# First batch in six transfers on two queues, feed-forward by rows of x, and casts of v in four pieces: an attention and GEGLU kernel

## The chip, the cores and the metric

One NeuronCore of a Trainium2 chip. The metric is the time of one execution in microseconds (us), as the device reports it. A profile is one execution with the hardware profiler on; its span is about 1.8 us shorter than the time reported for that execution. TensorE is PE in the profile, VectorE DVE, ScalarE ACT, GpSimd POOL, SyncE SP.

## The reference, cut to what matters

```python
q_s = softmax(q, over the 64 columns of a head)
k_s = softmax(k, over the 576 positions)        # written out with max and exp
kv  = einsum('bhsd,bhse->bhde', k_s, v)
x   = einsum('bhsd,bhde->bhse', q_s, kv)         # 8 batches, 8 heads, 576 positions, 64
x   = x.transpose(0, 2, 1, 3).reshape(4608, 512)
out = (gelu(x @ w_gate) * (x @ w_val)) @ w_out   # 512 -> 1536 -> 512, all float32
```

## The kernel before

The kernel works batch by batch. While PE does the feed-forward of batch b, the other engines prepare batch b+1: exp on ScalarE, sums and multiplies ("norm") on VectorE, the cast of v to 16 bits on GpSimd, and between feed-forward tiles PE does transposes (`unit_t`), K times V (`unit_kv`) and the products that give x (`unit_x`). Batch 0 has nothing to hide behind, so its start is exposed. Parts that the change touches (cuts marked `# ...`):

```python
def load(src, nm, b, h0, h1, n0):
    # ...
    for t in range(2):                       # even partitions, odd partitions
        nc.sync.dma_start(out=tiles[key][t:P:2, h0:h1, ...], in_=src[b, h0:h1]...)

def cast_v(b, h0, h1, eng="pool"):           # float32 -> float16
    copy_on(eng, v16_b[b % 2][:, :, h0:h1, 0:D]..., tiles[("v", b)][:, h0:h1, :]...)

def norm_mul(b, hp, eng="dve"):              # 128 x 640, both inputs in SBUF
    (nc.gpsimd if eng == "pool" else nc.vector).tensor_tensor(out=e, in0=e, in1=rrq..., op=ALU.mult)

def ffn_first(xt, after):                    # tiles by rows of x: rows 0,1 of all tiles, then 2, then 3
    # ...                                    # used for batch 1 only

for src, nm, n0 in ((q, "q", 1), (k, "k", 0), (v, "v", 0)):
    for h0 in (0, 4):
        load(src, nm, 0, h0, h0 + 4, n0)     # 12 transfers, all from SyncE; then the weights
# ...
warm_pe(14); norms of batch 0; unit_t(0, 0); warm_pe(4)
cast_v(0, 0, 4, "dve"); unit_t(0, 1); unit_kv(0, 0); warm_pe(2)
cast_v(0, 4, 6, "act"); cast_v(0, 6, 8, "dve")
unit_x(0, 0); unit_x(0, 1); unit_kv(0, 1); ... unit_x(0, 2); unit_x(0, 3)
```

`warm_pe(n)` runs n matmuls on zeros; it is meant to keep PE's clock up.

The softmax here doesn't subtract the row's maximum and nothing guards it: scores larger than these inputs give would overflow.

Of the kernel before, what the change touches and what calls it, by code (L numbers as in the profile page):

```python
# [18 lines left out]
def kernel(  # L19
# [10 lines left out]
    nc = tc.nc  # L30

    B, H, S, D = q.shape
# [65 lines left out]
    def load(src, nm, b, h0, h1, n0):  # L98
        key = (nm, b)
        if key not in tiles:  # L100
            tiles[key] = ldp.tile([P, H, NC * D], f32, name=f"{nm}t", tag="ld")
        for t in range(2):
            nc.sync.dma_start(  # L103
                out=tiles[key][t:P:2, h0:h1, n0 * D:NC * D],
                in_=src[b, h0:h1].rearrange("h (m n) d -> m h (n d)", n=NT)[
                    :, :, (4 * t + n0) * D:(4 * t + NC) * D])
# [10 lines left out]
    def copy_on(eng, dst, src):  # L117
        if eng == "pool":
            nc.gpsimd.tensor_copy(out=dst, in_=src)  # L119
        elif eng == "act":  # L120
            nc.scalar.copy(out=dst, in_=src)  # L121
        else:
            nc.vector.tensor_copy(out=dst, in_=src)  # L123

    def cast_w(nm, c, eng="pool"):
        dst = (wg_sb if nm == "wg" else wv_sb)[:, :, WCH[c]:WCH[c + 1]]
        copy_on(eng, dst, wst[(nm, c)])
# [11 lines left out]
    def exp(nm, b, h0=0, h1=H, n0=0, parts=((1, NC), (0, 1))):  # L139

        dst = (ek_b if nm == "k" else eq_b)[b % 2]
        for c0, c1 in parts if nm == "k" else ((n0, NC),):
            nc.scalar.activation(  # L143
                out=dst[:, c0:c1, h0 * D:h1 * D].rearrange("p n (h d) -> p h n d", d=D),
                in_=tiles[(nm, b)][:, h0:h1, c0 * D:c1 * D].rearrange("p h (n d) -> p h n d", d=D),
                func=ACTF.Exp, bias=kbias[:, 0:1] if c1 == 1 else 0.0)

    def cast_v(b, h0, h1, eng="pool"):
        copy_on(eng, v16_b[b % 2][:, :, h0:h1, 0:D].rearrange("p n h d -> p h n d"),
                tiles[("v", b)][:, h0:h1, :].rearrange("p h (n d) -> p h n d", d=D))  # L150

# [14 lines left out]
    def norm(b, hp, eng="dve", n0=0):  # L166
        norm_sum(b, hp, n0)
        norm_mul(b, hp, eng)
# [16 lines left out]
    def unit_kv(b, g):  # L185
        pskv = ps_att.tile([P, 2, 2 * VW], f32, name="pskv", tag="att")
        for j in range(2):
            hp = 2 * g + j
            for n in range(NC):
                nc.tensor.matmul(  # L190
                    pskv[:, j, :], ek_b[b % 2][:, n, hp * P:(hp + 1) * P],
                    v16_b[b % 2][:, n, 2 * hp:2 * hp + 2, 0:VW],
                    start=(n == 0), stop=(n == NC - 1))
        rck = att.tile([P, 2], f32, name="rck", tag="rck")
        nc.vector.reciprocal(out=rck, in_=pskv[:, :, D])
        for j in range(2):
            kv_sb = att.tile([P, 2, D], f16, name="kv_sb", tag="kv", bufs=12)
            nc.vector.scalar_tensor_tensor(  # L198
                out=kv_sb,
                in0=pskv[:, j, :].rearrange("p (h e) -> p h e", e=VW)[:, :, 0:D],  # L200
                scalar=rck[:, j:j + 1], in1=mask, op0=ALU.mult, op1=ALU.mult)
            st[(b, "kv", 2 * g + j)] = kv_sb

    def get_eqt(b):
        if (b, "eqt") not in st:
            st[(b, "eqt")] = att.tile([P, HP, S], f16, name="eqt", tag="eqt")
        return st[(b, "eqt")]

    def unit_t(b, g, eng="dve"):
        eqt = get_eqt(b)  # L210
        pst = ps_att.tile([P, 2, MAIN], f16, name="pst", tag="att")
        for j in range(2):
            hp = 2 * g + j
            for n in range(NM):
                nc.tensor.transpose(  # L215
                    pst[:, j, n * P:(n + 1) * P],
                    eq_b[b % 2][:, n + 1, hp * P:(hp + 1) * P], ident)
        copy_on(eng, eqt[:, 2 * g:2 * g + 2, 0:MAIN], pst)
# [14 lines left out]
    def get_xt(b):  # L233
        if (b, "xt") not in st:
            st[(b, "xt")] = att.tile([P, HP, MAIN], f16, name="xt", tag="xt")
        return st[(b, "xt")]

    def unit_x(b, hp, eng="act", big=False):
        xt = get_xt(b)
        psx = (ps_big if big else ps_att).tile([P, MAIN], f32, name="psx",  # L240
                                               tag="mm" if big else "att")
        nc.tensor.matmul(psx, st[(b, "kv", hp)].rearrange("p h e -> p (h e)"),  # L242
                         st[(b, "eqt")][:, hp, 0:MAIN], start=True, stop=True)
        copy_on(eng, xt[:, hp, :], psx)
# [8 lines left out]
    def warm_pe(n):  # L253
        ps = ps_big.tile([P, 512], f32, name="pswarm", tag="mm")
        for _ in range(n):
            nc.tensor.matmul(ps, ident, warm, start=True, stop=True)
# [5 lines left out]
    def mm_gv(ps, w, xt, fi, cis):  # L262
        for ci in cis:
            nc.tensor.matmul(ps, w[:, ci, fi * P:(fi + 1) * P], xt[:, ci, :],  # L264
                             start=(ci == 0), stop=(ci == HP - 1))

    def gate(psg, psv):
        gl = ffn.tile([P, 512], f32, name="gl", tag="gl")
        nc.scalar.activation(out=gl, in_=psg, func=ACTF.Gelu)  # L269
        ht = htp.tile([P, 512], f16, name="ht", tag="ht")  # L270
        nc.vector.scalar_tensor_tensor(  # L271
            out=ht, in0=psv, scalar=_H_SCALE, in1=gl, op0=ALU.mult, op1=ALU.mult)
        return ht
# [8 lines left out]
    def ffn_first(xt, after):  # L282

        ps = []
        for fi in range(len(after)):
            psg = ps_big.tile([P, 512], f32, name="psg", tag="mm")
            mm_gv(psg, wg_sb, xt, fi, range(0, 2))
            psv = ps_big.tile([P, 512], f32, name="psv", tag="mm")
            mm_gv(psv, wv_sb, xt, fi, range(0, 2))
            ps.append((psg, psv))  # L290
            for f in after[fi]:
                f()
        for fi, (psg, psv) in enumerate(ps):
            mm_gv(psg, wg_sb, xt, fi, [2])
            mm_gv(psv, wv_sb, xt, fi, [2])
        hts = []
        for fi, (psg, psv) in enumerate(ps):
            mm_gv(psg, wg_sb, xt, fi, [3])
            mm_gv(psv, wv_sb, xt, fi, [3])
            hts.append(gate(psg, psv))  # L300
        return hts
# [46 lines left out]


    for src, nm, n0 in ((q, "q", 1), (k, "k", 0), (v, "v", 0)):  # L350
        for h0 in (0, 4):
            load(src, nm, 0, h0, h0 + 4, n0)
    for c in range(NW):
        load_w_gv(c)
    for c in range(3):
# [17 lines left out]
    exp("q", 0, 4, 8, 1)  # L373
    exp("k", 0, 0, 4)
    exp("k", 0, 4, 8)
    warm_pe(14)
    norm(0, 0, "dve", 1)
    norm(0, 1, "pool", 1)
    norm(0, 2, "dve", 1)
    norm(0, 3, "pool", 1)  # L380
    unit_t(0, 0, "dve")
    warm_pe(4)
    cast_v(0, 0, 4, "dve")
    unit_t(0, 1, "dve")
    unit_kv(0, 0)
    warm_pe(2)
    cast_v(0, 4, 6, "act")
    cast_v(0, 6, 8, "dve")
    unit_x(0, 0, "act", True)
    unit_x(0, 1, "act", True)  # L390
    unit_kv(0, 1)
    cast_w("wg", 0, "pool")
    cast_w("wv", 0, "pool")
    unit_x(0, 2, "act", True)
    unit_x(0, 3, "dve", True)
    preload(ACTF.Gelu)
    for c in range(1, NW):
# [6 lines left out]
    FI, NS = 0, 1  # L404
    plan = {}

    def at(b, kind, i, *fns):
# [12 lines left out]
       L(preload, ACTF.Gelu))  # L420
    first1 = [[L(unit_kv, 1, 1), L(unit_t, 1, 1)], [L(unit_x, 1, 2, "act")],
              [L(unit_x, 1, 3, "dve")]]

    at(1, FI, 2, L(unit_trem, 1))
    at(1, FI, 3, L(exp, "q", 2), L(norm, 2, 0))
# [35 lines left out]
    def ride(b, kind, i):  # L461
        for fn in plan.get((b, kind, i), []):
            fn()

    for b in order:
        xt = get_xt(b) if b < B else xtr
        hts = []
        fi0 = 0
        if b == 1:
            hts = ffn_first(xt, first1)  # L470
            fi0 = 3
            ride(b, FI, 2)
        for fi in range(fi0, NFI):
            hts.append(ffn_fi(xt, fi))
            ride(b, FI, fi)
        if b == 0:
            psys = []
            for ns in range(4):
                psys.append(ps_big.tile([P, C], f32, name="psy", tag="mm"))
                mm_out(psys[ns], hts, ns, range(0, NFI // 2))  # L480
                ride(b, NS, ns)
            for ns in range(4):
                mm_out(psys[ns], hts, ns, range(NFI // 2, NFI))
                evac(b, ns, psys[ns])
                ride(b, NS, 4 + ns)
        else:
            for ns in range(4):
                psy = ps_big.tile([P, C], f32, name="psy", tag="mm")
                mm_out(psy, hts, ns, range(NFI))
                evac(b, ns, psy)  # L490
                ride(b, NS, ns)
# [30 lines left out]
```

## Time and profile before

| | before |
|---|---|
| time, three runs | 333.1 us median (332.79 to 333.62) |
| profiled execution | 332.57 us, span 330.8 |
| PE busy | 317.1 us, 96% |
| first feed-forward matmul | 18.39 us |
| rate of the transfers, 2 to 10 us | 263 GB/s, 388 later |

The lines themselves stand in the prediction. Reading hint: a PE matmul's record lasts 0.379 us, yet a row of 12 takes 2.59 us on the chain of waits, 0.216 each.

### The profile page before, as it was taken

To read this page: it belongs to the slowest core of one execution; us is meant where nothing else is said; L and a number is where in the kernel's file an instruction comes from. 1 tells how busy PE (TensorE), PEld (TensorE's weight loads), DVE (VectorE), ACT (ScalarE), POOL (GpSimd) and SP (SyncE) were. 2 spreads that over 40 slices of the span, in tenths; PEclk is the share of its full clock that TensorE was granted. 3 is DMA by queue.
4 is the path that set the end of the run, shared out by engine and by line. 5 is a ranking of instruction groups with operands and counts; after the bars stand their busy time and mean duration, and the time that the engine had idled before them with its cause. 6 is when DMAs were issued, how large, how long until landed. Compare 5 with 4: busy or idle time off the path is not lost.

```text
span 330.8 us, 4451 instructions
## 1 busy us (share of the span) xinstructions
PE 317.1 (96%) x1700; PEld 151.9 (46%) x1700; DVE 183.9 (56%) x327; ACT 146.7 (44%) x196; POOL 41.0 (12%) x40
## 2 busy tenths in 40 slices
PE   7699999997999999999999999999999999999994
PEld 2334444444455544544454445444544444444441
DVE  4743375499579736962599238832983234333331
ACT  3553564896353582349134932474243033103300
POOL 1377462211000200020002000200000000000000
PEclk9799999999999999999999999999999999999999
DMA  6999999970177015900491029301100110040002
GB/s 189 356 383 391 402 393 391 395 263 0 63 247 294 2 53 164 387 2 0 164 389 53 2 106 355 144 0 65 63 0 2 63 63 2 0 110 17 4 32 95
DMA packets 38453, 50.49 MB, mean 153 GB/s; under 512 B 2208, under 2 KB 34208, under 8 KB 38432
## 3 DMA queue, kind: packets, MB, share of 16 engines
q1 hardware_dynamic: 38288, 50.08, 42.7%
q8 instruction: 13, 0.21, 0.3%
q10 hardware_dynamic: 144, 0.13, 0.1%
q14 instruction: 8, 0.07, 0.1%
HBM read 40.76 MB, written 9.44 MB: 152 GB/s over the span
## 4 chain that ended last, share of the span: by engine, by line
PE 77%; DMA 9%; DVE 5%; ACT 3%; SPq 2%; issue 2%; POOL 1%; DVEq 0%; ACTq 0%; POOLq 0%
PE psy L308 26%; PE psg L264 23%; PE psv L264 22%; DMA wvst<-in_moe_w_val_dram 4%; DMA qt<-in_q_dram 3%; PE pskv L190 2%; DVE eq L163 2%; DMA kt<-in_k_dram 2%; PE psx L242 2%; PE pst L215 2%; DVE rq L156 1%; SPq L103 1%; ACT eq L143 1%; DVE ht L271 1%; ACT L143 1%
## 5 line engine op out<-in xcount | busy, mean ns | idle before, releaser
L269 ACT ACTIVATE gl<-psg 128x512 f32<-128x512 f32 x108 | 64.0, 598 | 140.3 <-PE psg L264 130.3
L271 DVE SCALAR_TENSOR_TENSOR ht<-psv,gl 128x512 f16<-128x512 f32 x108 | 73.8, 688 | 65.3 <-PE psv L264 61.0
L264 PE MATMUL psg<-xt,wg_sb 128*128 128x512 f16 x384 | 100.1, 379 | 0.7 <-ACT xt L121 0.5
L264 PE MATMUL psv<-xt,wv_sb 128*128 128x512 f16 x384 | 99.5, 379 | 0.1
L308 PE MATMUL psy<-wo_sb,ht 128*128 128x512 f16 x432 | 95.8, 379 | 0.0
L264 PEld LDWEIGHTS <-wv_sb 128*128 128x128 f16 x432 | 42.2, 98 | 51.9 <-issue 1.4
L308 PEld LDWEIGHTS <-ht 128*128 128x128 f16 x432 | 41.7, 98 | 48.4 <-DVE ht L271 0.2
L264 PEld LDWEIGHTS <-wg_sb 128*128 128x128 f16 x432 | 40.9, 98 | 45.0 <-issue 1.8
L342 DVE TENSOR_SCALAR yo<-psy 128x512 f32<-128x512 f32 x31 | 21.2, 687 | 48.6 <-PE psy L308 48.6
L119 POOL CAST v<-vt 128x2560 f16<-128x2560 f32 (+1 forms) x7 | 14.9, 2123 | 148.2 <-DMA vt<-in_v_dram 140.6
L156 DVE TENSOR_REDUCE rq<-eq 128x10 f32<-128x640 f16 (+1 forms) x32 | 25.4, 793 | 9.5 <-ACT eq L143 9.3
L163 DVE TENSOR_TENSOR eq<-eq,rrq 128x640 f16<-128x640 f16 (+1 forms) x27 | 26.0, 963 | 0.9
L121 ACT CAST xt<-psx 128x512 f16<-128x512 f32 x27 | 15.1, 587 | 16.8 <-PE psx L242 16.8
L143 ACT ACTIVATE eq<-qt 128x2560 f16<-128x2560 f32 (+1 forms) x9 | 18.5, 2051 | 4.7 <-DMA qt<-in_q_dram 4.6
L143 ACT ACTIVATE ek<-kt 128x2048 f16<-128x2048 f32 (+1 forms) x10 | 15.6, 1560 | 3.7 <-DMA kt<-in_k_dram 3.7
L215 PE MATMUL pst<-ident,eq 128*128 128x128 f16 x128 | 11.1, 226 | 4.9 <-DVE eq L163 2.8
L215 PEld LDWEIGHTS <-eq 128*128 128x128 f16 x128 | 8.7, 100 | 9.9 <-POOL eq L163 2.7
L190 PE MATMUL pskv<-v,ek 128*128 128x130 f16 x160 | 12.0, 220 | 1.2 <-DVE v L123 1.1
L190 PEld LDWEIGHTS <-ek 128*128 128x128 f16 x160 | 10.4, 97 | 4.7 <-issue 1.5
L264 PE MATMUL psg<-xtr,wg_sb 128*128 128x512 f16 x48 | 12.3, 379 | 0.0
L264 PE MATMUL psv<-xtr,wv_sb 128*128 128x512 f16 x48 | 12.3, 379 | 0.0
L242 PE MATMUL psx<-eqt,kv_sb 128*128 128x512 f16 x32 | 10.8, 380 | 1.1 <-DVE kv_sb L198 0.9
(52 smaller groups left out, 131.8 us busy)
## 6 DMA issues: line engine op xcount, KB each, us to landing
qt<-in_q_dram SPq DMA_DIRECT2D x14, 640.0 KB, 6.8
kt<-in_k_dram SPq DMA_DIRECT2D x12, 640.0 KB, 8.2
vt<-in_v_dram SPq DMA_DIRECT2D x12, 640.0 KB, 9.7
out_dram<-yo SPq DMA_DIRECT2D x14, 512.0 KB, 3.1
wost<-in_moe_w_out_dram SPq DMA_DIRECT2D x6, 512.0 KB, 8.8
kt<-in_k_dram SPq DMA_DIRECT2D x8, 320.0 KB, 6.8
vt<-in_v_dram SPq DMA_DIRECT2D x8, 320.0 KB, 6.6
wgst<-in_moe_w_gate_dram SPq DMA_DIRECT2D x5, 512.0 KB, 7.4
```

The lines of the kernel that those rows point to most:

```text
L121: nc.scalar.copy(out=dst, in_=src)
L143: nc.scalar.activation(out=dst[:, c0:c1, h0 * D:h1 * D].rearrange("p n (h d) -> p h n d", d=D), in_=tiles[(nm, b)][:, h0:h1, c0 * D:c1 * D ...
L156: nc.vector.reduce_sum(rq, e, axis=mybir.AxisListType.X)
L163: (nc.gpsimd if eng == "pool" else nc.vector).tensor_tensor(out=e, in0=e, in1=rrq.unsqueeze(-1).to_broadcast((P, n, 2, D)), op=ALU.mult)
L190: nc.tensor.matmul(pskv[:, j, :], ek_b[b % 2][:, n, hp * P:(hp + 1) * P], v16_b[b % 2][:, n, 2 * hp:2 * hp + 2, 0:VW], start=(n == 0), sto ...
L215: nc.tensor.transpose(pst[:, j, n * P:(n + 1) * P], eq_b[b % 2][:, n + 1, hp * P:(hp + 1) * P], ident)
L242: nc.tensor.matmul(psx, st[(b, "kv", hp)].rearrange("p h e -> p (h e)"), st[(b, "eqt")][:, hp, 0:MAIN], start=True, stop=True)
L264: nc.tensor.matmul(ps, w[:, ci, fi * P:(fi + 1) * P], xt[:, ci, :], start=(ci == 0), stop=(ci == HP - 1))
L269: nc.scalar.activation(out=gl, in_=psg, func=ACTF.Gelu)
L271: nc.vector.scalar_tensor_tensor(out=ht, in0=psv, scalar=_H_SCALE, in1=gl, op0=ALU.mult, op1=ALU.mult)
L308: nc.tensor.matmul(psy, hts[fi][:, ns * P:(ns + 1) * P], wo_sb[:, fi, :], start=(fi == 0), stop=(fi == NFI - 1))
L342: nc.vector.tensor_scalar(out=yo, in0=psy, scalar1=1.0 / _H_SCALE, scalar2=None, op0=ALU.mult)
```

## The change

The intent: bring in batch 0 sooner, start the feed-forward when two rows of x are there, and let VectorE through between GpSimd's casts of v. Its core:

```diff
-            nc.sync.dma_start(
+            eng = nc.scalar if b == 0 and t == 1 else nc.sync
+            eng.dma_start(
@@ cast_v
+        if eng == "pool" and h1 - h0 > 2:
+            for h in range(h0, h1, 2):
+                cast_v(b, h, h + 2)
+            return
@@ start
-        for h0 in (0, 4):
-            load(src, nm, 0, h0, h0 + 4, n0)
+        load(src, nm, 0, 0, H, n0)
-    warm_pe(14)
+    warm_pe(16)
-    warm_pe(4)
+    warm_pe(6)
     cast_v(0, 0, 4, "dve")
+    cast_v(0, 4, 6, "act")
     unit_t(0, 1, "dve")
+    cast_v(0, 6, 8, "pool")
     unit_kv(0, 0)
-    warm_pe(2)
-    cast_v(0, 4, 6, "act")
-    cast_v(0, 6, 8, "dve")
+    unit_kv(0, 1)
     unit_x(0, 0, "act", True)
     unit_x(0, 1, "act", True)
-    unit_kv(0, 1)
     ...
-    unit_x(0, 2, "act", True)
+    unit_x(0, 2, "dve", True)
@@ feed-forward
+    first = {0: [[], []], 1: first1}
-        if b == 1:
-            hts = ffn_first(xt, first1)
+        if b in first:
+            hts = ffn_first(xt, first[b])
```

More of the change, by code (lines that the diff above doesn't have):

```diff
@@ L468 @@
         fi0 = 0
-        if b == 1:
-            hts = ffn_first(xt, first1)
-            fi0 = 3
-            ride(b, FI, 2)
+        if b in first:
+            hts = ffn_first(xt, first[b])
+            fi0 = len(hts)
+            ride(b, FI, fi0 - 1)
         for fi in range(fi0, NFI):
```

## The prediction

> **What bounds the kernel now.** I read the page first. TensorE (PE) is busy nearly everywhere except at the very start, and the clock drops in one early slice; the DMA engines are full from the second slice to the seventh.
>
> ```profile
> PE   7699999997999999999999999999999999999994
> PEclk9799999999999999999999999999999999999999
> GB/s 189 356 383 391 402 393 391 395 263 0 63 247 294 2 53 164 387 2 0 164 389 53 2 106 355 144 0 65 63 0 2 63 63 2 0 110 17 4 32 95
> ```
>
> So time can come from few places. I asked for busy time in chosen stretches (time, then PE busy, PEld, DVE, ACT, POOL, clock, DMA share, GB/s). PE idles 2.2 us in 2 to 10, 1.5 in 10 to 15, 0.8 in 48 to 61, 1.9 in 61 to 92, 0.4 in 160 to 195, and almost nothing between these:
>
> ```profile
> 2.00:10.00 8.00, 5.79 (x22) 2.21 (x21) 3.86 (x10) 2.33 (x4) 1.04 (x1) 0.99 0.92 263
> 10.00:15.00 5.00, 3.47 (x24) 1.86 (x23) 3.41 (x6) 2.91 (x4) 1.04 (x1) 0.67 1.07 374
> 39.40:48.00 8.60, 8.51 (x46) 4.07 (x45) 5.06 (x10) 6.34 (x5) 4.79 (x5) 1.00 1.06 397
> 61.00:92.00 31.00, 29.13 (x166) 14.16 (x164) 22.63 (x38) 21.98 (x24) 4.37 (x2) 1.00 0.41 153
> 160.00:195.00 35.00, 34.58 (x195) 16.88 (x193) 22.41 (x37) 16.98 (x22) 2.33 (x1) 1.00 0.40 143
> ```
>
> Third, the chain of waits (start, length, what). Up to 39.5 us it runs through transfers, not through PE; then through the normalisation of batch 1 on VectorE and GpSimd; later it is PE, with two long VectorE pieces:
>
> ```profile
> 4.87 5.92 DMA kt<-in_k_dram
> 12.03 6.00 DMA wvst<-in_moe_w_val_dram
> 18.36 7.80 DMA wvst<-in_moe_w_val_dram
> 29.25 10.23 DMA qt<-in_q_dram
> 46.33 1.27 POOL eq L163
> 73.60 2.99 DVE eq L163
> 176.15 2.68 DVE eq L163
> ```
>
> Last, the timeline around the start and around those pieces. The rows below are, in order: the last cast of v for batch 0 (two), the first feed-forward matmuls, and the collision near 74 us with PE's wait for it.
>
> ```profile
> 15.08 0.73 ACT L121 CAST v<-vt 128x640 f16<-128x640 f32 x1 [1.89 <-DMA vt<-in_v_dram]
> 15.88 0.88 DVE L123 CAST v<-vt 128x640 f16<-128x640 f32 x1
> 18.39 1.32 PE L264 MATMUL psg<-xt,wg_sb 128*128 128x512 f16 x4
> 73.58 2.32 POOL L119 CAST v<-vt 128x2560 f16<-128x2560 f32 x1 [10.53 <-DMA vt<-in_v_dram]
> 73.60 2.98 DVE L163 TENSOR_TENSOR eq<-eq,rrq 128x640 f16<-128x640 f16 x1
> 76.64 0.40 PE L215 MATMUL pst<-ident,eq 128*128 128x128 f16 x4 [1.67 <-DVE eq L163]
> ```
>
> The same VectorE multiply takes 0.82 us everywhere else, so it lost 2.16 us here and 1.85 us at 176.15, each time to a GpSimd cast of v that started just before it (73.58, and 175.81). PE lost 1.67 us the first time and 0.42 us the second.
>
> **What the Trainium skill says.**
> 1. "SBUF — State Buffer", section "Who interferes with whom": VectorE and GpSimd share one port pair as an exclusive lock held for a whole instruction; a tensor_tensor with both inputs in SBUF contends with a GpSimd instruction that reads SBUF. The trace agrees: 2.98 us against 0.82 us, ending 0.6 us after the cast.
> 2. "DMA: Bandwidth & Descriptors", section "Issuing engines are not separate DMA queues": transfers from any engine run on the same 16 DMA engines; a second issuer saves only issue time. SyncE spends 0.77 us on the first issue and 0.61 to 0.62 on an unhindered one, here.
> 3. The same page, section "Queues, rings and completion order": a DMA engine takes turns between rings by packets, so two queues share rather than add. No run before shows two loading queues.
> 4. "TensorE: Matmul & The Clock Gate", section "Part 1: The HAM clock gate (the "warmup" mystery)": the clock halves after an idle window of about 3.4 us. The trace agrees in size: clock 0.93 in 9 to 10, 0.50 in 10 to 13, 0.87 in 13 to 14, about 3.4 us in all, following PE's gaps after its first 14 warming matmuls.
>
> **The change part by part.**
>
> *(a) Transfers.* Twelve issues become six, three on SyncE and three on ScalarE. For q, k and v each, the two cover odd and even partitions with all eight heads. Issue time for the batch falls from about 8.6 us on SyncE (0.74 to 9.3) to about 2 us on each queue. But issuing did not bind: transfers land 4 to 6 us after issue, so a backlog always waited. What is lost is rate: 263 GB/s from 2 to 10 us against 388 later, although the engines count as busy (0.92). In windows of one microsecond it is 276, 221 and 239 from 5 to 8, then 393 at 12. At 388 GB/s the 2.1 MB moved in those 8 us (8 times 263) take 5.4 us, so 2.6 us is the ceiling; about 1 us of it is the first transfers starting, which stays. I give the two queues half of the rest, some 0.8 us, because a slow packet in one ring need not hold up the other; that share is a guess. So v, 3.67 MB in all, should have landed at about 14.2 instead of just before 15.08. The price is that halves by heads are gone: the first exp on q, at 4.82 before, waits for all of q, say 6.5 to 7.5. The second exp, at 7.89 before, then follows 1.06 after the first, so its end, 8.95, hardly moves.
>
> *(b) Casts of batch 0's v.* All of v lands at once, and three engines cast: VectorE four heads (0.83), ScalarE two (0.73), GpSimd two (0.72, the size that it cast in batch 1 at 50.12). Before, VectorE's second cast sat behind a GpSimd weight cast, 0.88 us for half the size of one that took 0.83. Now GpSimd and VectorE meet again under the lock: together about 1.55 us.
>
> *(c) First two tiles by rows of x.* They start when two rows of x are there. Before, fi 0 started at 18.39 and fi 1 at 20.41, 2.02 us apart instead of 1.73 (8 matmuls of 0.216), so at most 0.3 us is to be had. After v lands: VectorE cast 0.93, ten matmuls 0.74, reciprocal and two products 0.8, product with queries and copy about 1.0, so first feed-forward matmul at about 3.4 us; before, 18.39 less 15.0 is also 3.4. Third tile: 16 matmuls later, 6.9 us after v instead of 22.14 less 15.0, 7.1. From the lock in (b) I take 0 to 0.7 back. So PE gains what v gains, about 0.8, plus 0.2, less 0.4: 0.6 us.
>
> *(d) Does it survive?* At 46.33 to 47.60 GpSimd multiplies batch 1's q, and PE starts the transposes on it at 47.64 after waiting 0.26 us. That piece hangs on q of batch 1, landed at 39.48 on a saturated stream. PE cannot pass it earlier than the stream advances, so (c) alone would be swallowed; what passes is the smaller of PE's and the stream's gain. The stream's is the 0.8 of (a). So 0.6 passes.
>
> *(e) GpSimd by head pairs.* Each whole-batch cast of 2.32 us becomes four of 0.72 (2.88, on an engine busy 12%). VectorE waits for one piece, up to 0.7, not 2.2. PE had 0.5 us of slack at 74 us (2.16 lost, 1.67 passed on) and 1.4 at 176 (1.85, 0.42). So nearly all of 1.67 plus 0.42 comes back: 2.0, less 0.2 for the piece that remains: 1.8 us. That VectorE gets in between two GpSimd instructions I take from the start: its cast at 15.88 ended at 16.76, between GpSimd casts started 15.80 and 16.53 (the latter took 0.69, not 0.61).
>
> *(f) Warming.* 20 small warm-up matmuls become 22; two between unit_kv calls go. On PE's idle time; no cost of their own.
>
> Sum: 0.6 plus 1.8 is 2.4 us less. I take off 0.3 for the rivals: 2.1, so 331.0 us.
>
> **The rivals.**
> - *The cold start stays.* The slow packets of the first 10 us belong to the memory, not to the queue, and two queues only interleave. For: the engines counted busy at 221 GB/s. Then (a), (c), (d) give 0 to 0.2, and (e) alone makes 331.3.
> - *The split casts hold on to the port.* If GpSimd runs its four back to back and VectorE gets no turn, VectorE would wait up to 2.9 us. Against: 15.88 above. Then 0.5 us worse at 74, and 333.0 or a little more.
> - *The clock.* Half clock in the window in which the feed-forward starts costs 1.2 to 1.7 us at the start. For: the warm-up inside the wait for v is gone and more waits stand together. Against: 22 warming matmuls. I give it 1 in 8; it would make 332.3.
> - *The collision moves by luck.* Cast and multiply met within 0.02 us at 74; in batches cast at 107.75, 142.44 and 211.78 VectorE was first and lost nothing. Any shift of the start could undo the 74 us stall without the split. This gives the same 331, for another reason.
> - *Two queues win all.* 1.6 us off the transfers and no lock: 329.8.
>
> **Range and chances.** The sum gives 331.0; the cold-start rival 331.3; the good case 329.8, with up to 0.5 for noise (three runs spread 0.8). Bad: 333.0. Range 329.5 to 333.1. Faster by over 2% needs under 326.4, a gain of 6.7, more than all idle PE time named above after 15 us plus the transfers' ceiling: 0.02. Slower by over 2% needs 339.8, several stalls at once: 0.01.
>
> **What would show it.** (a) the last cast of v in batch 0 starts near 14.2, GB/s in 2 to 10 rises above 290. (c) third tile's first matmul near 21.5. (d) q of batch 1 lands 0.5 to 1 us before 39.48. (e) no VectorE multiply of 640 columns over 1.6 us, PE idle in 61 to 92 under 0.5. Wrong if v lands after 14.9, if a multiply still takes 2.5, or if the clock shows 0.5 after 16 us.

## The result, and the profile after

| | before | after |
|---|---|---|
| time | 332.95 us median of 4 (332.37 to 333.62) | 329.31 us median of 4 (328.81 to 329.83) |
| profiled execution | 332.57, span 330.8 | 329.83, span 328.0 |
| PE busy | 317.1 | 317.6 |

The ratio is 0.989, 95% interval 0.9865 to 0.9915. Ratios here are the mean time of one kernel's fast runs over that of the other's of the same rounds, so not quite the ratio of the medians. The gain is 3.6 us where 2.1 was predicted; 329.31 lies 0.2 under the low end of the range.

The page after, the same three rows in 40 slices. PE's 7 in the tenth slice is gone. The clock's second slice has fallen from 7 to 5, and the transfers run at 236 and 375 GB/s in the first two slices instead of 189 and 356:

```profile
PE   7699999999999999999999999999999999999994
PEclk9599999999999999999999999999999999999999
GB/s 236 375 386 393 400 393 388 398 221 0 64 304 242 3 65 192 352 2 15 177 389 29 2 128 377 105 0 79 50 0 2 64 64 2 2 109 19 2 32 96
```

Busy time by stretch after (time, PE busy, PEld, DVE, ACT, POOL, clock, DMA share, GB/s). The stretch 61 to 92 lost 1.87 us of PE before and loses 0.33 now; 160 to 195 lost 0.42 and loses nothing. But 2 to 15 us is no better for PE, at clock 0.50 in the second row:

```profile
2.00:10.00 8.00, 5.56 (x19) 2.10 (x17) 2.58 (x6) 3.49 (x4) 0.00 (x0) 0.96 0.96 330
10.00:15.00 5.00, 3.65 (x17) 1.74 (x15) 4.67 (x9) 3.53 (x5) 2.95 (x3) 0.50 1.10 370
...
61.00:92.00 31.00, 30.67 (x177) 14.91 (x176) 20.76 (x37) 23.53 (x24) 4.25 (x6) 1.00 0.39 144
...
160.00:195.00 35.00, 35.00 (x197) 17.18 (x195) 20.78 (x38) 17.21 (x23) 3.34 (x4) 1.00 0.40 143
```

The chain of waits after (start, length, what). It no longer follows the transfers to 39.5 us: it leaves them at 6.7, goes through the preparation of batch 0, partly through six warm-up matmuls at half clock, and is on PE from there. The long VectorE piece at 73 us is 1.42, not 2.99:

```profile
0.74 5.97 DMA qt<-in_q_dram
...
10.52 1.05 POOL eq L168
...
12.23 2.56 PE pswarm L261 x6
...
39.40 7.77 PE psy L313 x36
...
73.25 1.42 DVE eq L168
```

The timeline after, at the start and at the former collision. All casts of v begin by 14.07, against 15.88 before. VectorE's takes 1.35 us where 0.83 is its own time, GpSimd's 1.31 for 0.72: they share the port, first with GpSimd's multiply that ran until 14.13. At 71.93 GpSimd casts in four pieces, and the multiply at 73.25 waits for one of them only; the eight transposes of PE follow with 0.27 us lost:

```profile
13.44 0.73 ACT L122 CAST v<-vt 128x640 f16<-128x640 f32 x1
13.46 1.35 DVE L124 CAST v<-vt 128x1280 f16<-128x1280 f32 x1
14.07 1.31 POOL L120 CAST v<-vt 128x640 f16<-128x640 f32 x1
...
18.39 0.72 PE L269 MATMUL psg<-xt,wg_sb 128*128 128x512 f16 x2
...
71.93 3.31 POOL L120 CAST v<-vt 128x640 f16<-128x640 f32 x4 [9.99 <-PE psv L269]
...
73.25 1.41 DVE L168 TENSOR_TENSOR eq<-eq,rrq 128x640 f16<-128x640 f16 x1
...
74.23 0.89 PE L220 MATMUL pst<-ident,eq 128*128 128x128 f16 x8
```

### The profile page after: what moved, and what is told of

Same layout as the page of the kernel before. It is cut to its first block, busy times and chain, and to the rows that moved or that the text cites. A ratio compares the mean times of both kernels' runs of the same rounds, so it can differ in the third digit from the quotient of the medians.

```text
span 328.0 us, 4481 instructions
## 1 busy us (share of the span) xinstructions
PE 317.6 (97%) x1702; PEld 153.0 (47%) x1702; DVE 180.7 (55%) x327; ACT 146.0 (44%) x195; POOL 46.3 (14%) x59
## 4 chain that ended last, share of the span: by engine, by line
PE 90%; DVE 4%; ACT 2%; DMA 2%; issue 1%; POOL 0%; DVEq 0%; ACTq 0%; POOLq 0%
PE psy L313 28%; PE psg L269 27%; PE psv L269 26%; PE pskv L195 3%; PE pst L220 2%; PE psx L247 2%; DMA qt<-in_q_dram 2%; DVE rq L161 1%; PE pswarm L261 1%; DVE eq L168 1%; DVE ht L276 1%; ACT eq L144 1%; PE pstr L232 1%; DVE kv_sb L203 0%; ACT L274 0%
## 5 line engine op out<-in xcount | busy, mean ns | idle before, releaser
L120 POOL CAST v<-vt 128x640 f16<-128x640 f32 x26 | 20.5, 828 | 140.9 <-DMA vt<-in_v_dram 63.9
L168 DVE TENSOR_TENSOR eq<-eq,rrq 128x640 f16<-128x640 f16 (+1 forms) x27 | 22.8, 845 | 0.9
L124 DVE COPY eqt<-pst 128x1024 f16<-128x1024 f16 x16 | 10.8, 678 | 0.9 <-PE pst L220 0.9
```

The source lines that it names most:

```text
L120: nc.gpsimd.tensor_copy(out=dst, in_=src)
```

## The experiments

Runs e1 to e4 shared one chip and 11 runs of before (332.7 us median, 331.07 to 333.99); e5 to e16 ran on another chip, in three sessions that share most of their 12 runs of before (332.54 us median, 331.83 to 333.93). e13 to e16 are single executions. All gave a correct result. The theory: the port's and the start's gains add, each of about 2 and 1 us. Rivals: the collision was luck of the trace; the transfers' rate belongs to the memory; the clock hides the start's gain.

### e1: the changed kernel again

No edit.

> The changed kernel once more, for its spread and for a second profile of its start. Main theory (start and split add, and the start depends on which clock window the first feed-forward matmuls meet): 3 to 4 us under before; the profile may show clock 0.5 in a different stretch than 9.6 to 16.4, and if it is back at 1.0 by 14 us, the output matmuls of batch 0 start about 1 us before 39.24. Rival (the first measurement was a lucky draw): 2 to 2.7 us, as the span of the first profile (2.75).

328.97 us (328.73 to 329.22), ratio 0.9888 (0.9865 to 0.9911). The size stands: 3.7 us, and it was not a lucky draw. In this trace the half clock came later and was shorter (12.35 to 15.76 us instead of 9.37 to 16.20), and the first feed-forward matmul came at 17.92 instead of 18.39.

### e2: the split alone

```diff
# kernel before, plus
+        if eng == "pool" and h1 - h0 > 2: ... cast_v(b, h, h + 2) ...
```

> Kernel before with nothing but the cast of v by head pairs on GpSimd. Main theory: 1.6 to 2.4 us under before, PE idle in 61 to 92 falls from 1.9 to about 0.3, no 640-column multiply over 1.5 us; nothing changes before 60 us. Rival (the collision at 74 us is luck of the profiled run, absent in most runs): under 1 us. Rival (GpSimd keeps the port through its four pieces): slower than before.

330.75 us, ratio 0.9944 (0.9918 to 0.9969), so 1.9 us. The port's part is real without any change of the start. Its profile happened to be its slowest run (331.63), and shows what the clock can do to a start. The rows are the stretches 10 to 15 and 15 to 20 us (the clock is the third number from the end), then the first feed-forward matmul, then the multiply:

```profile
10.00:15.00 5.00, 3.16 (x17) 1.74 (x18) 2.81 (x6) 2.91 (x4) 1.04 (x1) 0.50 1.07 368
15.00:20.00 5.00, 4.35 (x26) 2.73 (x27) 2.38 (x8) 1.80 (x3) 2.58 (x4) 0.58 1.08 334
```

```profile
20.14 1.32 PE L268 MATMUL psg<-xt,wg_sb 128*128 128x512 f16 x4
...
75.17 1.39 DVE L167 TENSOR_TENSOR eq<-eq,rrq 128x640 f16<-128x640 f16 x1
```

PE started at 20.14 instead of 18.39, 1.75 us later, with the same program at that place. Not all of this is the clock: the last of v landed at 15.55 instead of 15.01. From that landing to the first matmul it took 4.59 us instead of 3.38, so about 1.2 us go with the half clock, which lasted until 19.2 us here and until 13.3 in the first trace. Later this run wins 1.59 us between batch 1's first matmul and its first output matmul, and 0.61 in batch 4, although the multiply still met one piece of the cast: 0.82 of its own and 0.57 of waiting.

### e3: everything but the split

```diff
# changed kernel, minus
-        if eng == "pool" and h1 - h0 > 2: ...
```

> Changed kernel without the split. Main theory: 1.0 to 1.8 us under before, from the earlier transfers; at 74 us a whole cast may still hold a multiply for up to 2.2 us. Rival (collision by luck: a shifted start makes the multiply go first): 2.5 us or more under before, as much as with the split. Rival (start gains 0.3 only, as in the first profile): 0.3.

331.0 us, ratio 0.9957 (0.993 to 0.9984), so 1.4 us. Its trace has the multiply at 72.56 held for 2.49 us and PE waiting 1.18: a shifted start did not undo the collision here. Split alone and front alone, 1.9 and 1.4, make 3.3 of the 3.7.

### e4: the transfers alone

```diff
# kernel before, with
+            eng = nc.scalar if b == 0 and t == 1 else nc.sync
+        load(src, nm, 0, 0, H, n0)      # for the two calls by half heads
```

> Kernel before with nothing but the six transfers on two queues. Main theory: v landed by about 13.4 instead of 15.0 and q of batch 1 by about 38.1 instead of 39.5, as in the changed kernel, but PE's order of the start unchanged, so 0.3 to 1.0 us under before. Rival (rate of the cold start belongs to the memory): v lands at 14.9 or later, no gain. Rival (losing halves by heads delays q): 0.5 us slower.

331.48 us, ratio 0.9963 (0.9938 to 0.9988), 1.2 us. v landed at 12.98, q of batch 1 at 38.06. But batch 1's first matmul came at 52.19, no earlier than before (52.09): PE did not use it in this trace. What this execution won later was luck with the collision. The multiply near 74 us took 1.18 us, hardly held; but a later cast met another at 105, as the timeline shows:

```profile
105.17 2.33 POOL L120 CAST v<-vt 128x2560 f16<-128x2560 f32 x1 [30.97 <-DMA vt<-in_v_dram]
...
105.46 2.72 DVE L164 TENSOR_TENSOR eq<-eq,rrq 128x640 f16<-128x640 f16 x1
```

So the rival of luck holds in part: here a shift moved a collision to another place, and in the traces only the split made it cheap wherever it fell.

### e5, e6, e7: size or number of queues

```diff
# changed kernel, e5: the six transfers all from SyncE
-            eng = nc.scalar if b == 0 and t == 1 else nc.sync
# e6: twelve by half heads, still on two queues
+        for h0 in (0, 4): load(src, nm, 0, h0, h0 + 4, n0)
# e7: both, which is before's twelve from SyncE
```

> Changed kernel, the six transfers all on SyncE. If two queues are what removes the slow packets of the first 11 us: v lands near 15 again, rate in 2 to 10 us near 263 GB/s, and the kernel is 0.5 to 1.0 us slower than the changed one. If the size of the transfers does it: v by 13.6, rate near 330, same time as the changed kernel.

> Changed kernel with the twelve transfers by half heads, odd partitions still on ScalarE. If two queues do it: v by 13.6, the first half of q by 4.9, and at least as fast as the changed kernel (0 to 0.5 us faster). If the size does it: v near 15 and 0.5 to 1.0 us slower.

> Changed kernel with all of before's transfers (twelve, SyncE). Main theory (the start's gain is the transfers'): v at 15 to 15.5, 0.8 to 1.4 us slower than the changed kernel, so about as fast as the split alone, 1.9 to 2.6 under before. Rival (the row order and the new order of casts bring the start's gain): within 0.4 us of the changed kernel.

The stretch from 2 to 10 us (last number: GB/s), first of e5:

```profile
2.00:10.00 8.00, 5.83 (x19) 2.08 (x17) 2.69 (x6) 2.22 (x4) 0.00 (x0) 0.98 0.96 319
```

Then of e6:

```profile
2.00:10.00 8.00, 5.57 (x15) 1.86 (x13) 1.76 (x5) 3.77 (x5) 0.00 (x0) 1.00 0.98 321
```

And of e7:

```profile
2.00:10.00 8.00, 5.79 (x24) 2.27 (x23) 3.79 (x9) 2.39 (x5) 1.04 (x1) 1.00 0.89 265
```

| | twelve, one queue (before, e7) | six, one queue (e5) | twelve, two queues (e6) | six, two queues (after) |
|---|---|---|---|---|
| GB/s from 2 to 10 us | 263, 265 | 319 | 321 | 330 |
| last of v landed, us | 15.01, 15.27 | 14.09 | 14.05 | 13.36 |
| q of batch 1 landed, us | 39.48, 39.62 | 38.16 | 38.56 | 38.09 |
| time with all else changed, us | 330.06 (e7) | 329.66 | 330.17 | 328.97 (e1) |
| ratio to before | 0.9928 | 0.9922 | 0.9927 | 0.9888 |

Landings are those that the trace records. Neither pure theory holds: size alone and queues alone each bring v about 0.9 us earlier, both together 1.65. These are single traces; v landed at 14.70 to 15.55 in the five with the old transfers and at 12.98 to 13.36 in the eleven with the new ones, 1.95 apart on average. One rival was not tested: fewer transfers or two issuers also issue sooner. The last transfer of v was issued at 8.62 us in e7, 6.67 in e6, 4.24 in e5 and 2.45 in the changed kernel, which is nearly the order of the landings. So the runs do not tell whether size and queues act by themselves or through the earlier issue.

The times are less clear. The three variants lie about 1 us over the changed kernel, but that one ran in another session, and the intervals (0.9899 to 0.9945 for e5, 0.9865 to 0.9911 for e1) just overlap. On the chip of e5 to e7 the changed kernel was run twice, 329.64 and 329.42 (e15, e16), about as long as e5.

### e8 and e12: more warm-up

```diff
# changed kernel
-    warm_pe(16)
+    warm_pe(26)
```

> Changed kernel with 26 instead of 16 first warm-up matmuls, so that PE is busy until the first transposes near 9.6. If the half clock between 9.4 and 16 is what keeps PE from using the earlier v: no 0.5 in the clock, or only after 13, third tile's first matmul by 21.4 instead of 21.97, 0.3 to 0.7 us faster than the changed kernel. If the start is bound by VectorE, GpSimd and their port: no change within 0.2 us.

> The 26 warm-ups once more, in one session with the others: clock 1.0 throughout, 3.7 to 4.2 us under before, faster than the changed kernel's 328.97 by 0.2 to 0.5; runs spread less than the changed kernel's if the clock was what spread them.

328.65 us, ratio 0.9883 (0.9863 to 0.9903), and 328.85, ratio 0.9882 (0.9858 to 0.9905). The profile of e8 has full clock where the changed kernel had half; first the stretch 10 to 15, then the first matmuls of the feed-forward of batches 0 and 1:

```profile
10.00:15.00 5.00, 2.78 (x27) 1.58 (x25) 4.90 (x9) 3.53 (x5) 3.18 (x3) 1.00 1.10 369
```

```profile
17.32 0.72 PE L269 MATMUL psg<-xt,wg_sb 128*128 128x512 f16 x2
...
50.83 0.86 PE L269 MATMUL psg<-xt,wg_sb 128*128 128x512 f16 x2 [0.46 <-ACT xt L122]
```

PE is 1.07 us earlier than before in batch 0, and 1.26 in batch 1. That second number is exactly the advance of q of batch 1 (39.48 less 38.22, as the trace records it): in this run PE used all that the transfers had won. In e12 the same program got clock 0.66 in 10 to 15 and started at 17.94, so warm-ups of this number do not secure the clock, and its spread (328.41 to 329.24) is no smaller. Against 328.97 the gain is 0.1 to 0.3 us in medians: the lowest seen, but not told apart from the changed kernel.

The granted clock of each run, which the record lists, says more. Of the 13 runs with 26 warm-ups (e8, e11, e12), seven had a clock of 0.997 or 1.0 and took 328.41 to 328.67 us; six had 0.992 or 0.993 and took 328.80 to 329.35. Of the ten runs of the changed kernel (the result and e1) none had more than 0.993: eight with 0.992 or 0.993 took 328.73 to 329.22 us, two with 0.988 took 329.50 and 329.83. So the full clock was worth about 0.6 us, and it was met in seven of 13 runs with the longer warm-up and in none of ten without.

### e9: without the order by rows in batch 0

```diff
# changed kernel
-    first = {0: [[], []], 1: first1}
+    first = {1: first1}
```

> Changed kernel with batch 0's first two tiles each in one piece, as before. If the order by rows is worth what was predicted (at most 0.3): 0 to 0.4 us slower than the changed kernel, a gap of PE between the first two tiles. If it carries much of the start: over 0.8 us slower.

329.9 us, ratio 0.9912 (0.9893 to 0.9931); 0.9 us over e1's median, in another session. Batch 0's feed-forward takes 21.35 us from first matmul to first output matmul, against 20.85 in the changed kernel and 21.01 before: under the new order of casts the rows are worth 0.5 us, because the new order leaves the last two rows of x to VectorE, one after the other. The timeline of this run shows PE waiting for the fourth row. Three matmuls of 0.216 us from 18.73 end at 19.38, so from start to start 0.64 us are lost, not the 0.22 of the idle column:

```profile
18.73 1.06 PE L269 MATMUL psg<-xt,wg_sb 128*128 128x512 f16 x3
20.02 0.38 PE L269 MATMUL psg<-xt,wg_sb 128*128 128x512 f16 x1 [0.22 <-DVE xt L124]
```

### e10: v of batches 3 to 7 cast on ScalarE

```diff
# changed kernel
-    L(cast_v, b + 2, 0, H)
+    L(cast_v, b + 2, 0, H, "act")       # and the same for batch 3
```

> Changed kernel with the casts of v of batches 3 to 7 on ScalarE instead of GpSimd, so that from 60 us on only batch 2's cast can meet VectorE on the shared port. If the split has already given back nearly all that the port cost: within 0.4 us of the changed kernel, PE start-to-start of 61 to 195 the same to 0.3. If pieces still cost: faster by 0.5 or more. Rival: ScalarE's longer block delays the gelu and it is slower.

329.63 us, ratio 0.9907 (0.9889 to 0.9925): not faster. Batch 1 takes 24.65 us and batch 4 23.96, as in most traces of the changed kernel. The multiply near 73 us has its own 0.82 us back, but there was nothing left to win.

### e11: more warm-up, and batch 0's last cast of v on ScalarE

```diff
# changed kernel
+    warm_pe(26)
+    cast_v(0, 6, 8, "act")
```

> Changed kernel with 26 first warm-up matmuls and batch 0's last v cast on ScalarE instead of GpSimd, which takes that cast off the shared port. Theory (the start is capped by the transfer stream: q of batch 1 lands near 38.2): PE may start the feed-forward 0.3 us earlier than with the warm-ups alone, but the second batch's start stays at 50.8, so within 0.3 us of the next run. Rival (PE's own start sets the end): 0.3 to 0.5 faster.

328.8 us, ratio 0.9885 (0.9867 to 0.9903), against 328.85 for e12 beside it. First matmul at 17.81 and batch 1 at 51.05, 0.13 and 0.14 earlier than in e12. The times show no difference.

### e13 to e16: two more traces of each kernel

No edits; e13 and e14 are before (332.28 and 331.81 us), e15 and e16 the changed kernel (329.64 and 329.42).

> Kernel before, a second trace. If the collisions are fixed by the order of work: the same multiplies held near 74 and 176 us, batch 1's feed-forward 26.3 to 26.7 us and batch 4's 24.4 to 24.7 from its first matmul to its first output matmul. Rival (luck): one of them absent. The start: v at 15 or later, batch 1's first matmul between 51.9 and 53.7, following the clock's half windows.

> Kernel before, a third trace; the same expectations as for the second.

> Changed kernel, a third trace: v by 13.5, batch 1's first matmul between 50.8 and 51.8, batch 1's feed-forward 24.6 to 25.0 us, batch 4's 23.9 to 24.1.

> Changed kernel, a fourth trace; the same expectations as for the third.

From the timelines, per trace: batch 1's first feed-forward matmul; from it to the first output matmul of batch 1; the same for batch 4; the end of the last matmul to the end of the span; the span.

| us | start of batch 1 | batch 1 | batch 4 | close | span |
|---|---|---|---|---|---|
| before | 52.09 | 26.51 | 24.57 | 4.40 | 330.79 |
| e13 | 52.01 | 26.33 | 24.54 | 4.39 | 330.50 |
| e14 | 52.91 | 25.17 | 24.30 | 4.39 | 330.00 |
| mean before | 52.34 | 26.00 | 24.47 | 4.39 | 330.43 |
| after | 51.74 | 24.94 | 23.97 | 4.17 | 328.04 |
| e1 | 51.27 | 24.66 | 23.97 | 4.15 | 327.28 |
| e15 | 51.84 | 24.66 | 23.97 | 4.17 | 327.86 |
| e16 | 51.61 | 24.66 | 23.97 | 4.16 | 327.62 |
| mean after | 51.62 | 24.73 | 23.97 | 4.16 | 327.70 |
| difference | 0.72 | 1.27 | 0.50 | 0.23 | 2.73 |

All that is not in these columns agrees to 0.02 us. So the whole gain of the traced executions is: start 0.72, port 1.77, close 0.23. For the start alone there are more traces, since up to batch 1 the program of e2 is that of before, and those of e3 and e10 are that of the changed kernel. With them batch 1 starts at 52.67 us on average of four and at 51.46 on average of six: a gain of 1.2 us. This may be a little much, as e2's trace was the slowest run of its kernel.

Not all came as expected. e14 had v at 14.70, before the 15 expected, and batches 1 and 4 under the ranges given; e15 started batch 1 at 51.84, 0.04 over its range. The collisions occur in each trace of before, but not alike. In e14 PE was late at the start (half clock until 19.1 us, first row below, and 4.69 us from the last of v to the first matmul), VectorE with it, and only the end of the cast met the multiply:

```profile
15.00:20.00 5.00, 4.33 (x22) 2.20 (x20) 2.37 (x8) 2.19 (x5) 3.41 (x5) 0.59 1.11 372
...
73.06 2.33 POOL L119 CAST v<-vt 128x2560 f16<-128x2560 f32 x1 [10.22 <-PE psv L264]
...
74.42 1.64 DVE L163 TENSOR_TENSOR eq<-eq,rrq 128x640 f16<-128x640 f16 x1
...
76.12 0.40 PE L215 MATMUL pst<-ident,eq 128*128 128x128 f16 x4 [0.34 <-DVE eq L163]
```

This also answers why time lost at the start of before does not simply add: e14 started 0.82 us later than the first trace and still ended 0.79 us earlier.

## Why the prediction was right or wrong

The direction, the two places and the mechanism of the split were right; the size was too small, 2.1 for 3.6, and the range missed by 0.2. The steps that failed are sizes in the sum: the start's 0.6, of which 0.7 to 1.2 was measured, for reasons partly wrong ((a), (c)); the 0.3 taken off for rivals, of which nothing was measured; and a close of 0.23 that had no term. Together they make 0.6 to 1.1 of the 1.5 us that were missing. The rest stays open.

**(a), transfers: mis-sized.** 0.8 us for v, measured 1.65 (15.01 to 13.36), 1.95 on average of all traces; the rate rose to 330, over the 290 asked for. The step that failed is "I give the two queues half of the rest": it counted the second queue alone, and six transfers on one queue (e5) gain about as much as twelve on two (e6). The reason given, that a slow packet in one ring need not hold up the other, is shown by no run. The rival "the cold start stays", which gave the start 0 to 0.2, is refuted. The price named there was paid: the first exp on q began at 6.79, in the 6.5 to 7.5 given.

**(b), casts of batch 0: right, a little short.** VectorE and GpSimd met under the port, 1.35 and 1.31 us; both were done 1.92 us after the first began, not 1.55, since GpSimd's multiply held the port first.

**(c) and (d): about right or too small, and for a partly wrong reason.** 0.6 was to pass, and 0.72 passes on average of the table (0.35 in the first trace), 1.2 with the larger set. "PE gains what v gains" failed. It kept 3.4 us from the last of v to the first feed-forward matmul. In the six traces of the changed start this took 4.56 to 5.33 us, so in the first of them the first matmul came at 18.39, no earlier than before, and the third tile's at 21.97, where 21.5 was given and 22.14 was measured before. The chain after shows what took the rest: the multiply on GpSimd, the half clock and six warm-ups at 0.43 us each, so "no cost of their own" in (f) did not hold there. With full clock (e8) it took 4.20. And 3.4 was itself one trace of before: with the long half clock of e2 and e14 it took 4.59 and 4.69. The order by rows was sized right: batch 0's feed-forward took 21.01 or 21.02 us in the three traces of before and 20.74 to 20.85 after, so 0.2; e9's 0.5 is against the new order of casts. That the stream caps PE in batch 1 held: in all eighteen traces batch 1 starts at least 12.61 us after its q has landed, and before, e7 and e8 stand at that bound.

**(e), the split: right sum, wrong parts.** 1.8 predicted, 1.77 on average. But the parts were misread. PE's loss was taken from the idle column, 1.67 and 0.42. Here are the transposes just ahead of the first wait, in the timeline of before, and four transposes on its chain of waits:

```profile
74.58 0.39 PE L215 MATMUL pst<-ident,eq 128*128 128x128 f16 x4
```

```profile
59.51 0.22 PE pstr L227 x4
```

Four transposes hold PE up for 0.22 us, so the next could start at 74.80; it started at 76.64, which makes 1.84, not 1.67. The idle column starts counting only when the record ends, 0.17 us later, since a record includes the time in which later matmuls may already run. In batch 4 it is 178.06 plus 0.22 against 178.87, so 0.59, not 0.42. The loss of that one trace was thus 2.43, and against e1, where no piece got in the way, the stretches indeed differ by 1.85 and 0.60. The other way, one trace was taken for the kernel: in e14 batch 1 lost only 0.51 against 24.66. The two errors cancel in the mean. "0.2 for the piece that remains" was right where it occurs: 0.28 in the first trace after, nothing in the three others. That VectorE gets in between two pieces was right: in the thirteen traces with the split no such multiply took over 1.41 us.

**The discount for rivals: wrong.** 0.3 was taken off; against before, nothing was lost to them on average. The clock rival did occur, but in both kernels. In before's start it cost about 1.2 us in two of four traces (e2, e14). In the changed kernel its sign, half clock after 16 us, came in three of four traces, which had it until 16.20 (the first) and 16.83 (e15, e16); e8 takes 0.8 to 1.1 us less from v to the first matmul. The prediction's 3.4 us of half clock, which it set beside the skill's idle window, is how long the half clock lasted, and not an idle time of PE.

**What was not in the sum.** 0.23 us after the last matmul. From the last matmul to the end it takes 4.39 to 4.65 us in the five traces without the split (before, e13, e14, e3, e4) and 4.00 to 4.18 in the thirteen with it. In the traces looked at closely the difference is a pause of GpSimd among its closing instructions (0.40 us in the first trace of before, 0.04 in the first after). Why was not tested.

**What stays open.** The sum of measured terms is 2.7 us, which is the difference of the traced executions, or 3.2 with the larger set of starts; the timed ones differ by 3.6 and 3.7, with an interval of some 0.8 to either side. The traced executions of before (332.57, 332.28, 331.81) all lie under its median of 332.95. Those of the changed kernel (329.83, 329.07, 329.64, 329.42) mostly lie over its 329.31. A late clock together with a full collision would make an execution of 334, as in the upper end of before's runs (333.99), and after the split the collision no longer adds. That is argued from e2 and the table; no trace shows such an execution. The range had 0.5 us for noise and was drawn around one profile, and it should have been wider on the side of the gain: two costs that vary by 1 us each, the clock and the collision, were both in before, and the change removes one of them.

## What to carry to other kernels

Read a wait's cost on PE from start to start against an undisturbed stretch, not from the idle column, and look at more than one execution before a cost that depends on a meeting of two engines is put into a sum. Where two engines share a port and work in the background meets work in front, cutting the background instruction into pieces can bound the loss by one piece: here it was 0.59 us at most in thirteen traces, wherever the meeting fell. A start that is moved forward gains only as far as the next thing it waits for, here the clock, the port and the stream of the following transfers. The clock at the start differs from run to run, so a start should be compared over several traces.

## What the Trainium skill lacked or had wrong

- "DMA: Bandwidth & Descriptors", "Issuing engines are not separate DMA queues": it says that a second issuer saves only issue time, which is usually small. In the first 10 us here, the rate with the second queue was 321 GB/s instead of 265 with twelve transfers (e6, e7), and 330 instead of 319 with six (after, e5). Whether the queue or the earlier issue did it is not shown, but the saving was not small.
- No page speaks of the low rate of the first microseconds: 263 to 281 GB/s from 2 to 10 us in the five traces with twelve transfers on one queue (before, e2, e7, e13, e14), 388 later; larger transfers alone made it 319.
- "SBUF — State Buffer", "Who interferes with whom": the lock and the waiting agree. What it does not say is who comes next when one engine has several instructions queued: VectorE's multiply got in after one piece of four, with 1.41 us instead of 2.98, and none took longer in the thirteen traces with the split.
- "TensorE: Matmul & The Clock Gate", Part 1, puts the ramp's cost at under 1% of a typical span and advises not to fit a particular count of slow matmuls. About 1.2 us in one execution here (e2), 0.4%, agrees with that, but it is a third of what the change gained: too much to leave out when a change is this small.
